# Attention followed by a squared-ReLU layer: filler count, order of the v load, two-part AV and an undrained batch change

## The chip, the cores and the metric

The kernel runs on one core of one Trainium2 chip. Its engines are TensorE (PE, the matmuls; PEld is its weight load, which runs beside the matmuls), VectorE (DVE), ScalarE (ACT), GpSimd (POOL) and SyncE (SP, which issues DMAs). The metric is device time of one launch in microseconds (us), the median of several runs. A profile is taken from one execution; its span is the time from the first to the last instruction.

## The reference

```
scores = (q @ k^T) / sqrt(64)            # 8 batches, 16 query heads, 4 key heads, 384 tokens, 64 wide
attn   = softmax(scores)
x      = (attn @ v), heads side by side  # 3072 x 1024
h      = relu(x @ w_in)                  # w_in 1024 x 2048
out    = (h * h) @ w_out                 # w_out 2048 x 1024
```

## The kernel before, in words

A *pair* is two query heads of one batch that share a key head; a batch has 8 pairs, and there are 64 pairs, numbered n = 0 to 63. The feed-forward part of a batch is 16 *up* chunks (x times 128 columns of w_in, L616) and two *down* halves of w_out, each with three row tiles (L642).

Three styles of code follow one another.

**The first batch (the prologue)** is cut into 24 units (one pair by 128 queries) and is ordered by a small planner (L107). Each task has an assumed duration, an earliest time (K_AT, Q_AT, V_AT at L794 to L796 say when loads are taken to have landed; W_AT and B_AT when further loads are issued) and takes buffers from pools. The planner's output is a static order for each engine. Where TensorE's assumed clock shows a gap, the hook `between` (L861) puts in *fillers*: matmuls on a zero tile (L313) whose results nobody reads. A unit is: scores (L395), exp on ScalarE (L406), AV (L422, attention weights times v, with a column of ones that gives the row sums), and for each two units a division (L431, L433) and a transpose back (L332, L444). The first 4 up chunks of batch 0 are done here for each of three row tiles t (L447: four matmul groups into PSUM bank `f_ps[0]`, then relu L460 and square L465). Keys and queries are cast (L300, L305) and transposed on TensorE (L332, L340). The first loads are issued by hand on SP and ACT (L278 to L287): k of group 0, q of pairs 0 and 1, k of the other groups, v, then q of pairs 2-3, 4-5, 6-7.

**From batch 1 on** TensorE is used as two halves of 64 rows, *lo* and *hi*, that work at the same time: every product is cut into pieces for the lower and the upper 64 rows of the contraction. `push` (L502) emits the lo pieces at once and keeps the hi pieces in the list `behind`; `catch_up` (L482) emits them among later lo pieces, at the earliest GAP = 450 ns of assumed clock after the lo pieces end, since the hi pieces add to the same PSUM bank and the first of them waits for the last lo piece. A job marked urgent goes ahead of others. `drain` (L525) emits all hi pieces that are left, with no lo work beside them. `both` (L518) emits pieces on both halves. `next_bank` (L535) hands out four PSUM banks in rotation (`rota`).

For each pair n there are: first half of its scores (L545; three matmuls into banks 0 to 2, then one exp L557 over the three), second half of its scores into the same three banks, so that it has to wait for the first exp; AV of pair n-1 (`row_attend`, L561: 18 lo pieces, then 18 hi pieces, all into the one bank `po`, then reciprocal L575 and multiplication L577 on VectorE, which free `po` and fill `o_sb`); and steps of the feed-forward part, taken one by one from the generator `ffn` (L740). An up step ends in relu (L629) and a square; a down tile is computed in three steps of 6, 5 and 5 matmuls per half for each of three tiles, after which VectorE copies it out (L664).

**Batch 1** (n = 8 to 15, L882 to L895) has a hand-written order per pair: first scores, one ffn step, `row_turn(n-2)` (L591: o_sb transposed on TensorE, then copied to xT at L607), AV of pair n-1, second scores, one ffn step. The 16 ffn steps are the 12 up chunks of batch 0 that are left and the first four steps of its first down half (9 steps in all).

**The batch change** (n = 16, L896 to L904): AV of pair 15, ffn step, turn of pair 14, ffn step, turn of pair 15, then `fill(LULL)` takes ffn steps for 6000 ns, then `drain()`, and only then the scores of pair 16. From there pairs go on with `fill(ahead)` and `fill(per - ahead)` (2200 and 2800 ns) between the halves of the scores; transposes are done by DMA. The keys and queries of batch 2 are transposed by DMAs from SP (L359, L366), issued in pair 13. After the last pair the rest of the feed-forward part runs with full 128-row matmuls (L684, L703).

Of the kernel before, what the change touches and what calls it, by code (L numbers as in the profile page):

```python
# [165 lines left out]
def bass_gqa_attention__then__ffn_squared_relu_kernel(  # L166
# [106 lines left out]
    def first_q(c0, c1, queue):  # L273
# [6 lines left out]
    first_q(1, 2, "sync")  # L280
    first_k(1, 4)
    R.add("sync", lambda e: e.dma_start(
        v_f.ap().rearrange("p g j d -> p g (j d)"), v[0].rearrange("g (p j) d -> p g (j d)", j=NJ)),
        writes=["v_f"], dma="vf")
    first_q(2, 4, "sync")
    first_q(4, 6, "sync")
# [153 lines left out]
    def unit_turned(u, bank):  # L440
# [4 lines left out]
              reads=[key], writes=[("xT", 0, c, t), ("xT", 0, c + 1, t)])  # L445

    def unit_up(t, c):  # L447
        acc, key = f_ps[0].ap(), ("f_ps", 0)

        def mm(pe):  # L450
            for kc in range(NKC):
                m = pe.matmul(acc[:, c * 128:(c + 1) * 128], w_in_sb[:, kc, c * 128:(c + 1) * 128],  # L452
                              xT[0][:, kc, t * 128:(t + 1) * 128], start=(kc == 0), stop=(kc == NKC - 1))
            return m

        R.add("tensor", mm, reads=[("w_in", c * 128 // WC)] + [("xT", 0, kc, t) for kc in range(NKC)], writes=[key])

    def unit_relu(t):
        acc, key = f_ps[0].ap(), ("f_ps", 0)
        R.add("vector", lambda e: e.tensor_scalar_max(hq[t % 2][:, :], acc, 0.0),  # L460
              reads=[key], writes=[("hq", t % 2)] + under(t % 2))
# [69 lines left out]
    held = set()  # L531
    rota = [0, 1, 2, 3]
    po_owner = []
# [26 lines left out]

    def row_attend(p, then=None):  # L561
        b, g = p // NPB, (p % NPB) // 2
# [21 lines left out]

        while po_owner and not po_owner[-1]["over"]:
            clock["lo"] += 100.0
            catch_up(clock["lo"])
        lo, hi = ([piece(r, f, j) for f in range(2 * NJ) for j in range(NJ)] for r in range(2))
        po_owner.append(push(lo, hi, done, urgent=True)[0])

    def row_turn(p):  # L591
        b, c = p // NPB, p % NPB
        i = next_bank()
        acc, key = F_BANKS[i]
        ps = acc.bitcast(bf16)
# [18 lines left out]
        owner[i], total = push(lo, hi, done, urgent=True)  # L614

# [202 lines left out]
    for u in range(NU):  # L818
# [6 lines left out]
        if c % 2 == 0:  # L825
            acc = {}
        av[u] = P.task(on_pe(0.19), lambda e, h, u=u, ex=slot: unit_attend(u, h["bank"], ex["exp"]), 1 + u * 0.01,
                       [a, v_cast] + ([av[u - 1]] if c % 2 else []), take=[] if c % 2 else ["bank"],
                       give=[("exp", slot)], hold=acc)
        if c % 2:  # L830
# [8 lines left out]
                       give=[("bank", b2), ("ob", o)], hold=b2)  # L839
            a["give"].append(("bank", acc))  # L840
            turned_at[t].append(x)
    done = None
    W_LAND = 15.0
    for t in range(NJ):
        up_hold, hq_hold, a = {}, {}, None
        for c in range(4):
            a = P.task(on_pe(0.45), lambda e, h, t=t, c=c: unit_up(t, c), 20 + t, turned_at[t] + ([a] if a else []),
                       take=[] if c else ["up"], hold=up_hold, at=W_LAND if c < 2 else W_LAND + 2.8)
        a = P.task({DVE: (0.69, 0.03)}, lambda e, h, t=t: unit_relu(t), 13, [a], take=["hq"], give=[("up", up_hold)],
                   hold=hq_hold)  # L850
        P.task({POOL: (1.05, 0.03)}, lambda e, h, t=t: unit_square(t), 5, [a], give=[("hq", hq_hold)], hold=hq_hold)
# [21 lines left out]
    for n in range(NPB, NP + 1):  # L873
# [78 lines left out]
```

## Time and profile before

| | |
|---|---|
| median of 3 runs | 433.91 us (433.33 to 434.0) |
| the profiled execution | 433.79 us |
| its span, first to last instruction | 431.9 us |
| TensorE busy | 423.8 us (98%) |
| VectorE, ScalarE, GpSimd busy | 166.7, 198.0, 60.8 us |
| first scores of pair 8 (end of the prologue) | 33.20 us after the span's start |
| second scores of pair 16 | 81.41 us |

A timeline row reads: start, duration, engine, line, operation, output<-inputs, shape, count of merged instructions; in brackets the idle time of the engine before it and what ended it. A row of a waits view reads: who <- whom: us in total, times, longest. In a groups view the figures after the bar are busy us and mean ns of one. Matmul ends are modelled, so a matmul row is longer than the time it keeps others out: starts are the better measure.

### The profile page before, as it was taken

The numbers are of one execution on the slowest core, as the hardware profiler recorded it, in microseconds if no ns is written. First come the engines' busy times: TensorE is split into PE (matmuls) and PEld (weight loads), VectorE is DVE, ScalarE is ACT, GpSimd is POOL, SyncE is SP. The second block draws the span as 40 slices with busy tenths as digits, with TensorE's granted clock in tenths as the row PEclk, the third lists the DMA queues.
The fourth block names the chain that finished last, engine by engine and source line by source line (L and its number), as shares of the span: only waits on it lengthen the run. The fifth ranks groups of instructions, "written<-read, shape, count | busy, mean of one in ns | idle before, by whom it ended". The sixth has DMA issues, their size and how long they took to land.

```text
span 431.9 us, 13352 instructions
## 1 busy us (share of the span) xinstructions
PE 423.8 (98%) x6173; PEld 319.9 (74%) x6173; DVE 166.7 (39%) x364; ACT 198.0 (46%) x250; POOL 60.8 (14%) x75
## 2 busy tenths in 40 slices
PE   8999998899999999999999999999999999999997
PEld 6786675678878888888788887888878888746544
DVE  4773543242333442344422543334423444224412
ACT  4945550565333564436644565445654466003300
POOL 4927350021000300022000300021000000000000
PEclk9999999999999999999999999999999999999999
DMA  7999999139521990249603992239902210120012
GB/s 218 178 197 201 202 190 184 43 34 153 157 69 61 132 175 20 93 103 147 94 20 94 115 184 45 80 63 171 123 20 94 83 21 20 45 97 26 0 61 86
DMA packets 92792, 44.25 MB, mean 102 GB/s; under 512 B 71104, under 2 KB 86720, under 8 KB 92736
## 3 DMA queue, kind: packets, MB, share of 16 engines
q0 software_dynamic: 34288, 16.65, 30.9%
q1 hardware_dynamic: 58176, 26.55, 29.3%
q8 instruction: 48, 0.79, 0.7%
q10 hardware_dynamic: 272, 0.20, 0.1%
q14 instruction: 8, 0.07, 0.1%
HBM read 35.65 MB, written 12.58 MB: 112 GB/s over the span
## 4 chain that ended last, share of the span: by engine, by line
PE 93%; DVE 2%; ACT 2%; DMA 2%; SPq 0%; issue 0%
PE f_ps L655 15%; PE f_ps L623 15%; PE sc_ps L655 14%; PE sc_ps L623 14%; PE po L567 11%; PE f_ps L703 7%; PE sc_ps L553 7%; PE f_ps L684 5%; DMA q_f<-in_q_dram 2%; ACT expT L557 2%; PE f_ps L452 1%; PE sc_ps L395 1%; PE po L422 0%; PE f_ps L332 0%; PE f_ps L422 0%; DVE q_f L664 0%
## 5 line engine op out<-in xcount | busy, mean ns | idle before, releaser
L557 ACT ACTIVATE expT<-sc_ps 128x1152 bf16<-128x1152 f32 x112 | 126.2, 1126 | 99.9 <-PE sc_ps L553 50.0
L623 PE MATMUL sc_ps<-xT,w_in_sb 64*128 64x384 bf16 x864 | 133.8, 322 | 0.4 <-DVE q_f L664 0.4
L655 PE MATMUL f_ps<-w_out_sb,h2T 64*128 64x512 bf16 x640 | 131.7, 376 | 0.0
L623 PE MATMUL f_ps<-xT,w_in_sb 64*128 64x384 bf16 x864 | 130.7, 323 | 0.2 <-DVE q_f L664 0.2
L655 PE MATMUL sc_ps<-w_out_sb,h2T 64*128 64x512 bf16 x608 | 128.2, 376 | 0.0
L623 PEld LDWEIGHTS f_ps<-xT,w_in_sb 64*128 64x128 bf16 x864 | 71.3, 94 | 16.1 <-DVE q_f L664 0.9
L623 PEld LDWEIGHTS sc_ps<-xT,w_in_sb 64*128 64x128 bf16 x864 | 71.4, 94 | 15.5 <-DVE q_f L664 0.9
L635 ACT ACTIVATE h2T<-hr 128x384 bf16<-128x384 f32 x96 | 50.1, 522 | 71.5 <-DVE hr L629 71.5
L567 PE MATMUL po<-v_aug,expT 64*128 64x65 bf16 x2016 | 81.4, 190 | 1.0 <-DVE o_sb L577 1.0
L567 PEld LDWEIGHTS po<-v_aug,expT 64*128 64x128 bf16 x2016 | 75.9, 94 | 8.7 <-DVE o_sb L577 1.3
L655 PEld LDWEIGHTS f_ps<-w_out_sb,h2T 64*128 64x128 bf16 x640 | 56.0, 94 | 12.5 <-PE sc_ps L655 0.6
L655 PEld LDWEIGHTS sc_ps<-w_out_sb,h2T 64*128 64x128 bf16 x608 | 54.4, 94 | 12.0 <-PE f_ps L655 0.3
L553 PE MATMUL sc_ps<-qT,kT 64*128 64x384 bf16 x336 | 55.2, 323 | 1.7 <-ACT expT L557 1.2
L575 DVE RECIPROCAL rinv<-po 128x6 f32<-128x6 f32 x56 | 11.0, 196 | 104.4 <-PE f_ps L655 47.4
L629 DVE TENSOR_SCALAR hr<-sc_ps 128x384 f32<-128x384 f32 x54 | 30.0, 556 | 36.2 <-PE sc_ps L623 24.0
L629 DVE TENSOR_SCALAR hr<-f_ps 128x384 f32<-128x384 f32 x54 | 30.1, 558 | 33.6 <-PE f_ps L623 19.5
L577 DVE TENSOR_TENSOR o_sb<-po,rinv 128x384 bf16<-128x384 f32 x56 | 31.2, 557 | 1.9
L703 PE MATMUL f_ps<-w_out_sb,h2T 128*128 128x512 bf16 (+2 forms) x160 | 31.5, 358 | 0.0
L553 PEld LDWEIGHTS sc_ps<-qT,kT 64*128 64x128 bf16 x336 | 23.8, 94 | 8.4 <-ACT expT L557 5.2
L234 POOL DMA_DIRECT2D k_st<-in_k_dram x7 | 5.3, 760 | 170.2 <-DMA xT<-o_sb 170.2
L703 PEld LDWEIGHTS f_ps<-w_out_sb,h2T 128*128 128x128 bf16 x160 | 15.0, 98 | 16.5 <-DVE q_f L664 0.4
L693 ACT ACTIVATE h2T<-hr 128x384 bf16<-128x384 f32 x16 | 8.4, 523 | 33.7 <-DVE hr L691 33.7
(84 smaller groups left out, 253.0 us busy)
## 6 DMA issues: line engine op xcount, KB each, us to landing
out_dram<-q_f SPq DMA_DIRECT2D x47, 256.0 KB, 2.3
q_st<-in_q_dram POOLq DMA_DIRECT2D x7, 768.0 KB, 11.1
w_in_sb<-in_moe_w_in_dram POOLq DMA_DIRECT2D x8, 512.0 KB, 14.5
w_out_sb<-in_moe_w_out_dram POOLq DMA_DIRECT2D x2, 2048.0 KB, 23.2
k_st<-in_k_dram POOLq DMA_DIRECT2D x7, 192.0 KB, 4.5
v_st<-in_v_dram POOLq DMA_DIRECT2D x7, 192.0 KB, 10.8
q_f<-in_q_dram SPq DMA_DIRECT2D x3, 384.0 KB, 7.4
xT<-o_sb SPq DMA_TRANSPOSE x48, 2.7
```

Of the source, the lines that this page charges most:

```text
L553: "tensor", lambda pe: pe.matmul(sc_ps[:, i, 0:S], kt[rows, j * 128:(j + 1) * 128], qt[rows, :]),
L557: R.add("scalar", lambda e: e.activation(expT[p % NEX][:, 3 * half:3 * half + 3, :], sc_ps[:, 0:3, 0:S], AF.Exp, scale=0.125), reads=[("sc ...
L567: "tensor", lambda pe: pe.matmul(po_v[:, f % NJ, f // NJ, :], expT[p % NEX][rows, 2 * j + f % 2, f // 2 * 128:f // 2 * 128 + 128], v_aug[b ...
L575: R.add("vector", lambda e: e.reciprocal(rinv_v, po_v[:, :, :, D:D + 1]), reads=["po"], writes=[("rinv", p % 2)])
L577: R.add("vector", lambda e: e.tensor_tensor(o_sb[p % NO][:, :, :, :], po_v[:, :, :, 0:D], rinv_v.to_broadcast([128, NJ, 2, D]), ALU.mult), ...
L623: "tensor", lambda pe: pe.matmul(acc[:, 0:S], w_in_sb[rows, kc, c * 128:(c + 1) * 128], xT[b % NXT][rows, kc, :], start=(h == 0 and kc == ...
L629: R.add("vector", lambda e: e.tensor_scalar_max(hr[r][:, :], acc[:, 0:S], 0.0), reads=[key], writes=[("hr", r)])
L635: R.add("scalar", lambda e: e.activation(h2T[b % 2][:, c, :], hr[r][:, :], AF.Square), reads=[("hr", r)], writes=[("h2T", b % 2, c, t) for ...
L655: "tensor", lambda pe: pe.matmul(acc, h2T[b % 2][rows, c, i * 128:(i + 1) * 128], w_out_sb[rows, c, jj * 512:(jj + 1) * 512], start=(h == ...
L684: m = pe.matmul(acc[:, 0:S], w_in_sb[:, kc, c * 128:(c + 1) * 128], xT[b % NXT][:, kc, :], start=(kc == 0), stop=(kc == NKC - 1))
L693: R.add("scalar", lambda e: e.activation(h2T[b % 2][:, c, :], hr[r][:, :], AF.Square), reads=[("hr", r)], writes=[("h2T", b % 2, c, t) for ...
L703: m = pe.matmul(f_ps[u][:, 0:c1 - c0], h2T[b % 2][:, c, i * 128:(i + 1) * 128], w_out_sb[:, c, jj * 512 + c0:jj * 512 + c1], start=(c == 0 ...
```

## The change

- **Fillers.** Eight instead of six at the start; the planner's TensorE clock is then set to 2.8 us instead of staying at 1.4. In gaps before 5.2 us a filler counts as 0.22 us, later as 0.11; before, 0.13 throughout.
- **Loads.** The load of v is issued after that of q pairs 2-3. The planner's landing times for k, q and v and the issue time of w_in are set later (v at 9.1 instead of 6.9; q pairs 2-3 at 7.85 instead of 8.2).
- **Planner.** A pool `acc` of two limits how many AV accumulators hold a bank at once. The up chunks of the last row tile (t = 2) go to bank 3 of `sc_ps` instead of `f_ps[0]`; the rotation starts at bank 1 accordingly.
- **AV of batch 1's loop in two parts.** `row_attend(p, part=0)` does 9 lo and 9 hi pieces, `part=1` the other 9 and 9 after them, then the division. The order per pair is: first scores, ffn step, AV part 0 of n-1, second scores, turn of n-2, ffn step, AV part 1 of n-1.
- **Batch change.** Two ffn steps, turn of 14, AV of 15 (whole), two ffn steps, turn of 15 into the bank `po`, `fill(LULL)`; no drain.

```diff
     first_k(1, 4)
+    first_q(2, 4, "sync")
     R.add("sync", lambda e: e.dma_start(
         v_f.ap()...
-    first_q(2, 4, "sync")
...
+    def up_bank(t):
+        return (f_ps[0].ap(), ("f_ps", 0)) if t < NJ - 1 else (sc_ps[:, 3], ("sc", 3))
+
     def unit_up(t, c):
-        acc, key = f_ps[0].ap(), ("f_ps", 0)
+        acc, key = up_bank(t)
...
     def unit_relu(t):
-        acc, key = f_ps[0].ap(), ("f_ps", 0)
+        acc, key = up_bank(t)
...
-    rota = [0, 1, 2, 3]
+    rota = [1, 2, 3, 0]
...
-    def row_attend(p, then=None):
+    def row_attend(p, then=None, part=None):
...
-        while po_owner and not po_owner[-1]["over"]:
-            clock["lo"] += 100.0
-            catch_up(clock["lo"])
-        lo, hi = ([piece(r, f, j) for f in range(2 * NJ) for j in range(NJ)] for r in range(2))
-        po_owner.append(push(lo, hi, done, urgent=True)[0])
-
-    def row_turn(p):
+        if part != 1:
+            while po_owner and not po_owner[-1]["over"]:
+                clock["lo"] += 100.0
+                catch_up(clock["lo"])
+        heads = range(NJ) if part == 0 else range(NJ, 2 * NJ) if part == 1 else range(2 * NJ)
+        lo, hi = ([piece(r, f, j) for f in heads for j in range(NJ)] for r in range(2))
+        prev = po_owner.pop() if part == 1 else None
+        po_owner.append(push(lo, hi, None if part == 0 else done, prev, urgent=True)[0])
+
+    def row_turn(p, home=None):
         b, c = p // NPB, p % NPB
-        i = next_bank()
-        acc, key = F_BANKS[i]
+        if home is None:
+            i = next_bank()
+        acc, key = home or F_BANKS[i]
...
+    P.pool("acc", range(2))
...
-    K_AT = (3.3, 5.6, 5.6, 5.6)
-    Q_AT = (3.9, 4.5, 8.2, 8.2, 9.4, 9.4, 10.6, 10.6)
-    V_AT = 6.9
+    K_AT = (3.3, 6.2, 6.2, 6.2)
+    Q_AT = (3.9, 4.5, 7.85, 7.85, 10.35, 10.35, 11.6, 11.6)
+    V_AT = 9.1
...
-    W_AT, B_AT = 7.0, 12.0
+    W_AT, B_AT = 8.0, 12.0
...
         if eng == PE and was < 16.0 and begin - was > 0.3:
-            idle(int((begin - was - 0.1) / 0.13))
-
-    idle(6)
+            idle(int((begin - was - 0.1) / (0.22 if was < 5.2 else 0.11)))
+
+    idle(8)
+    P.clock[PE] = 2.8
...
             row_scores(n, 0)
             next(ffn)
+            if n > NPB:
+                row_attend(n - 1, part=0)
+            row_scores(n, 1)
             if n > NPB + 1:
                 row_turn(n - 2)
+            next(ffn)
             if n > NPB:
-                row_attend(n - 1)
-            row_scores(n, 1)
-            next(ffn)
+                row_attend(n - 1, part=1)
...
         if n == 2 * NPB:
+            next(ffn)
+            next(ffn)
+            row_turn(n - 2)
             row_attend(n - 1)
             next(ffn)
-            row_turn(n - 2)
             next(ffn)
-            row_turn(n - 1)
+            row_turn(n - 1, (po.ap(), "po"))
             ready[0] = 1
+            credit[0] = 0.0
             fill(LULL)
-            drain()
```

More of the change, by code (lines that the diff above doesn't have):

```diff
@@ L613, in row_turn @@
             catch_up(clock["lo"])
-        owner[i], total = push(lo, hi, done, urgent=True)
+        job, total = push(lo, hi, done, urgent=True)
+        if home is None:
+            owner[i] = job
     def row_up(b, c, r):
@@ L827, in bass_gqa_attention__then__ffn_squared_relu_kernel @@
         av[u] = P.task(on_pe(0.19), lambda e, h, u=u, ex=slot: unit_attend(u, h["bank"], ex["exp"]), 1 + u * 0.01,
-                       [a, v_cast] + ([av[u - 1]] if c % 2 else []), take=[] if c % 2 else ["bank"],
+                       [a, v_cast] + ([av[u - 1]] if c % 2 else []), take=[] if c % 2 else ["bank", "acc"],
                        give=[("exp", slot)], hold=acc)
@@ L839, in bass_gqa_attention__then__ffn_squared_relu_kernel @@
                        give=[("bank", b2), ("ob", o)], hold=b2)
-            a["give"].append(("bank", acc))
+            a["give"] += [("bank", acc), ("acc", acc)]
             turned_at[t].append(x)
@@ L847, in bass_gqa_attention__then__ffn_squared_relu_kernel @@
             a = P.task(on_pe(0.45), lambda e, h, t=t, c=c: unit_up(t, c), 20 + t, turned_at[t] + ([a] if a else []),
-                       take=[] if c else ["up"], hold=up_hold, at=W_LAND if c < 2 else W_LAND + 2.8)
-        a = P.task({DVE: (0.69, 0.03)}, lambda e, h, t=t: unit_relu(t), 13, [a], take=["hq"], give=[("up", up_hold)],
-                   hold=hq_hold)
+                       take=["up"] if c == 0 and t < NJ - 1 else [], hold=up_hold, at=W_LAND if c < 2 else W_LAND + 2.8)
+        a = P.task({DVE: (0.69, 0.03)}, lambda e, h, t=t: unit_relu(t), 13, [a], take=["hq"],
+                   give=[("up", up_hold)] if t < NJ - 1 else [], hold=hq_hold)
         P.task({POOL: (1.05, 0.03)}, lambda e, h, t=t: unit_square(t), 5, [a], give=[("hq", hq_hold)], hold=hq_hold)
```

## The prediction, made before the changed kernel ran

> **What bounds the kernel now.** I read the page first, then the waits of TensorE, then a table of stretches, then the timeline row by row where that table shows TensorE short of work.
>
> ```profile
> span 431.9 us, 13352 instructions
> PE 423.8 (98%) x6173; PEld 319.9 (74%) x6173; DVE 166.7 (39%) x364; ACT 198.0 (46%) x250; POOL 60.8 (14%) x75
> PE 93%; DVE 2%; ACT 2%; DMA 2%; SPq 0%; issue 0%
> ```
>
> TensorE is the bound: no other engine is half busy, and 93% of the chain that ended last is its own. So the change can only win where TensorE waits or runs one half alone. The execution took 433.79 us, 1.9 us more than its span; the median is 433.91, so the sum below holds for either.
>
> ```profile
> 33.20:63.05 29.85, 29.42 (x537) 20.04 (x536) 13.65 (x30) 16.97 (x15) 18.10 (x20) 1.00 1.36 203
> 63.05:81.41 18.36, 15.18 (x205) 9.10 (x199) 6.24 (x13) 3.72 (x5) 0.00 (x0) 1.00 0.88 144
> 81.41:102.00 20.59, 20.59 (x337) 16.36 (x339) 8.21 (x17) 12.97 (x19) 4.20 (x4) 1.00 0.60 56
> ```
>
> The columns are the stretch, its length, and the busy time of PE, PEld, DVE, ACT and POOL. From 81.41 on TensorE is full, and nothing of the change acts there. The stretch of the batch change (second scores of pair 15 to second scores of pair 16) has 3.2 us without any matmul. The loop of batch 1 looks full, but a busy half counts as busy, so I check it by starts below.
>
> **Part 1, the prologue.** Engines are mixed in this timeline of before:
>
> ```profile
> 1.05 4.96 PE L316 MATMUL f_ps<-warm 128*128 128x256 bf16 x24 [1.05 <-DVE tiny L290]
> 3.28 0.55 DVE L305 CAST k_dup<-k_f 128x384 bf16<-128x384 f32 x1 [2.28 <-DMA k_f<-in_k_dram]
> 5.85 0.33 PE L332 MATMUL sc_ps<-ident,k_dup 128*128 128x128 bf16 x3
> 6.90 0.51 PE L395 MATMUL sc_ps<-qT,kT 64*128 64x128 bf16 x12
> 7.29 3.65 ACT L406 ACTIVATE expT<-sc_ps 128x768 bf16<-128x768 f32 x5 [4.57 <-PE sc_ps L395]
> 8.37 0.83 POOL L309 CAST v_aug<-v_f 128x768 bf16<-128x768 f32 x1 [1.06 <-DMA v_f<-in_v_dram]
> 9.54 1.05 DVE L300 CAST q_st<-q_f 128x384 bf16<-128x384 f32 x2 [0.78 <-DMA q_f<-in_q_dram]
> 21.80 4.83 ACT L406 ACTIVATE expT<-sc_ps 128x768 bf16<-128x768 f32 x6 [0.18 <-PE sc_ps L395]
> 31.31 1.96 PE L452 MATMUL f_ps<-xT,w_in_sb 128*128 128x128 bf16 x32 [0.26 <-DVE q_f L460]
> ```
>
> The first keys are cast at 3.83, but their transpose starts at 5.85, since 24 fillers stand ahead of it: 4.8 us for 24 is 0.20 us each, where the planner counted 0.13. In the changed kernel the planner's gap from 2.8 to the cast's planned end at 3.95 takes (1.15 - 0.1)/0.22 = 4 fillers, 12 in all. At 0.21 us each they end at 3.6, and the transpose starts when the cast is done, about 3.9. From there to the first exp before took 7.29 - 5.85 = 1.44 us; at the slow pace and with the query's transpose behind its cast I take 2.0, so the first exp comes at 5.9, **1.4 us earlier**.
>
> Not all of that arrives. Two pairs give six units, which last the exps from 5.9 to about 10.7 (24 exps end at 26.63, so 0.81 apart). Queries 2-3 now load in the place of v: they land near 8.3 instead of 9.5, so they come in time, but v lands near 9.5 instead of 8.3, so with a cast of 0.83 the first AV starts near 10.4, where before the cast had ended at 9.2. Two AVs are thus owed, the planner assumes both landings 0.4 us too early, and TensorE executes in order, so it stands at them. I take 0.5 us off. Against that, the own bank of t = 2 removes the 0.26 us wait at 31.31 for the relu of t = 1. Sum: 1.4 - 0.5 + 0.2 = **1.1 us gained**, from 0 (the AVs owed cost the lead) to 2.0 (all of it, and half of the exps' idle time between). The pool of two accumulators I cost at nothing: an AV that it delays is covered by the 9 exp buffers.
>
> [...]
>
> ```profile
> L316 PE MATMUL f_ps<-warm 128*128 128x256 bf16 x20 | 4.4, 420 | 1.1 <-DVE tiny L290 1.1
> L316 PE MATMUL f_ps<-warm 128*128 128x256 bf16 x3 | 0.5, 272 | 0.0
> ```
>
> The first row (from 1 to 5.2 us) has fillers of 420 ns, the second (at 6.2 us) the same ones at 272 ns, so TensorE ran slow until about 5.5 us. The changed kernel leaves gaps of up to 0.3 us unfilled from 3.6 on. [...]
>
> **Part 2, batch 1's loop.** One full pair of before, TensorE, ScalarE and VectorE:
>
> ```profile
> 46.28 0.29 PE L567 MATMUL po<-v_aug,expT 64*128 64x65 bf16 x4
> 46.81 0.32 PE L553 MATMUL sc_ps<-qT,kT 64*128 64x384 bf16 x1
> 47.45 1.13 ACT L557 ACTIVATE expT<-sc_ps 128x1152 bf16<-128x1152 f32 x1 [1.23 <-PE sc_ps L623]
> 48.41 0.20 DVE L575 RECIPROCAL rinv<-po 128x6 f32<-128x6 f32 x1 [0.71 <-PE f_ps L623]
> 48.64 0.56 DVE L577 TENSOR_TENSOR o_sb<-po,rinv 128x384 bf16<-128x384 f32 x1
> 48.63 0.49 PE L553 MATMUL sc_ps<-qT,kT 64*128 64x384 bf16 x3
> 50.35 0.29 PE L567 MATMUL po<-v_aug,expT 64*128 64x65 bf16 x4
> 52.71 0.49 PE L553 MATMUL sc_ps<-qT,kT 64*128 64x384 bf16 x3
> ```
>
> ```profile
> 36.64 0.50 PE sc_ps L553 x3
> 40.48 0.50 PE sc_ps L553 x3
> 60.82 0.50 PE sc_ps L553 x3
> 81.91 1.30 PE sc_ps L623 x16
> 103.78 1.08 PE f_ps L655 x10
> ```
>
> From first scores to first scores is 52.71 - 48.63 = 4.08 us. The work of one half: an up step is 1.30 (16 pieces on two halves, in the chain of waits), the scores 0.49, AV 18 x 0.033 = 0.59, a turn 0.09; with two up steps 3.77. So **0.31 us a pair is lost**, and the rows say where: second scores at 46.81, exp at 47.45 for 1.13, next first scores at 48.63. This round trip of 1.82 us has only one up step beside it.
>
> The split moves half an AV (0.30) and the turn into that gap: 0.16 + 0.09 + 1.30 + 0.30 = 1.85, so that wait goes. **But a new one comes.** Part 0 of the next pair writes the same bank `po` and must wait for the division, and this distance shrinks. Before, from AV start to AV start there were 50.35 - 46.28 = 4.07 us, of which the round trip needs 49.20 - 46.28 = 2.92. At the batch change the trace shows that it can bite:
>
> ```profile
> 62.54 0.22 PE L567 MATMUL po<-v_aug,expT 64*128 64x65 bf16 x2
> 65.03 0.56 DVE L577 TENSOR_TENSOR o_sb<-po,rinv 128x384 bf16<-128x384 f32 x1
> 65.65 0.20 PE L567 MATMUL po<-v_aug,expT 64*128 64x65 bf16 x1 [1.04 <-DVE o_sb L577]
> ```
>
> Here two AVs stand close, and the second starts 3.11 us after the first, with 1.04 us of idle TensorE. Half an AV takes 0.30 off the lo run and 0.30 off the hi run, not off the gap between them nor off VectorE's 0.79: from part 1 to the next part 0 it needs 2.39 (from 2.92, and 0.06 to get back) to 2.52 (from 3.11). What stands between is 0.30 + 0.32 + 1.30 = 1.92. So TensorE waits 0.47 to 0.60 us in each pair; I take 0.50. Queued behind the waiting piece are the rest of the AV and the second scores, on both halves, so it is a plain loss. Part 1's own wait for part 0's last hi piece costs nothing: 1.4 us needed, 1.85 there. A pair then takes 3.77 + 0.50 = **4.27 instead of 4.08**.
>
> Counted over the loop: pair 8 is unchanged; pair 9 (40.48 - 36.64 = 3.84) has no division ahead and takes 0.32 + 1.30 + 0.30 + 0.16 + 1.30 + 0.30 = 3.68 or a little more, 0.14 less; pairs 10 to 14 took 60.82 - 40.48 = 20.34 and will take 21.35; pair 15 up to its second scores (at 63.05) took 2.23 and will take 1.62 + 0.50 + 0.30 = 2.43. **1.05 us lost**, where a split without the new wait would gain 1.8.
>
> **Part 3, the batch change.**
>
> ```profile
> 69.01 0.20 PE L601 MATMUL sc_ps<-ident,o_sb 64*128 64x64 bf16 x1 [0.36 <-DVE xT L607]
> 72.89 0.33 PE L623 MATMUL sc_ps<-xT,w_in_sb 64*128 64x384 bf16 x1 [0.38 <-DVE q_f L664]
> 78.39 0.33 PE L553 MATMUL sc_ps<-qT,kT 64*128 64x384 bf16 x1
> 80.25 1.11 ACT L557 ACTIVATE expT<-sc_ps 128x1152 bf16<-128x1152 f32 x1
> 81.41 0.50 PE L553 MATMUL sc_ps<-qT,kT 64*128 64x384 bf16 x3 [1.23 <-ACT expT L557]
> ```
>
> The work of one half between the two second scores: scores 0.16 and 0.32, six down steps at 1.08, AV 0.59, two turns 0.18, four up steps 5.20: 12.93 us of 18.36, so **5.43 us are lost**. Named: 1.04 (AV of 15 at `po`), 0.36, 0.38, and 1.23 for the exp, which came late because drained squares stood ahead of it on ScalarE and only one up step stood between the score halves. The other 2.4 is one half working alone, in the drain above all.
>
> In the new order AV of 15 has two down steps ahead of it (2.46 against 2.39 needed: no wait), turn of 15 has two after the AV (0.59 + 2.16 = 2.75 against 3.05: 0.3 us of wait, new, since it needs `o_sb` and `po`); the first up chunk needs the copied xT only at its last piece, 2.2 us after the turn, where some 1.4 is enough. No up step waits for a copied-out down bank, since the turn no longer takes one and four up steps spread the rest. After LULL two up steps (2.6) stand between the score halves instead of one, more than the 1.82 needed. The same work then takes 12.93 + 0.3, and 0.39 for half an AV and a turn that now fall behind the mark: 13.62, **4.74 us gained**. The credit line does nothing, since credit is 0 there already.
>
> What could come late instead is the DMA of batch 2's queries:
>
> ```profile
> 62.03 10.21 SPq L366 DMA_TRANSPOSE qT<-q_st  x2
> DMA to landing us min/median/max: 11.0/11.0/11.0
> ```
>
> The first transpose lands at 73.0; pair 16's first scores move from 78.39 to about 76, so 3 us are left.
>
> **Sum:** 433.79 - 1.1 + 1.05 - 4.74 = **429.0 us**.
>
> **The rivals.**
> *The division is no wait* (hi pieces or VectorE quicker than in the rows): the loop gains 1.8 instead of losing 1.05, 426.2. For it: 0.31 a pair is there to be had. Against: 2.92 and 3.05 in the rows above. Chance 0.20.
> *The batch change does not do what it says*: only the waits of 1.04 and 1.23 go, and what the drain cost comes back as waits for banks and xT. 433.79 - 1.1 + 1.05 - 2.3 = 431.4. Chance 0.13.
> *The prologue's lead is lost* at the later v: 430.1, chance 0.08. With the second rival at once, and 0.60 for each wait in the loop, 433.1: within the noise, chance 0.06.
> *Slower: TensorE does not reach full pace in the prologue.* Its work there, counted by starts, is about 19 us of the 27.3 from 5.9 to 33.2 (24 units and 24 transposes with 0.17 for a group, 12 up groups at 0.45). At half pace all of it takes 38 us, and the loop begins 9 to 11 us later: 439. The point: x us at half pace cost 0.29x, so slower than before needs some 19 us of it. For it: 272 against 420 ns above. Against: full pace came after 4.5 us, and the new gaps are short. [...]
>
> **How the numbers follow.** The forecast has 0.45. The range 425.6 to 431.6 takes in the forecast with both ends of part 1, the wait from 0 to 0.60, and the first three rivals (0.86); the last two cases lie outside. A measurement of this kernel tells about 0.2% (0.9 us) from no change. Faster: 0.45 + 0.20 + 0.13 + 0.08 = 0.86; same 0.06; slower 0.08.
>
> **What would show it.** First exp near 5.9 and first scores of pair 8 near 32.1; rows of L567 with a wait of about 0.5 on DVE o_sb L577 in pairs 10 to 15, and 4.27 from first scores to first scores; no wait of the second scores of pair 16 for the exp. A period of 3.8 would make part 2 wrong, a wait on DMA qT part 3, fillers' pace lasting beyond 6 us part 1.

## The result, and the profile after

The changed kernel took **430.19 us** (median of 6 runs, 429.58 to 430.39) against 434.04 for the kernel before on the same chip (6 runs, 433.33 to 435.27): the medians are 3.85 us apart, and the ratio is 0.9903, 95% interval 0.9886 to 0.9920, so about 1% faster. The forecast was 429.0 with a range of 425.6 to 431.6. The sign and the size are right, but three terms of the sum are not. Their errors (1.1 and 0.8 us too much gained, 0.76 too much lost) cancel in part, so that the sum came within 1.2 us is in part luck. The profiled execution took 430.17 us.

The first three lines of the page after, as they stood for before (length; busy time of the engines; the chain that ended last):

```profile
span 428.3 us, 13436 instructions
PE 421.3 (98%) x6215; PEld 329.9 (77%) x6215; DVE 167.3 (39%) x366; ACT 197.7 (46%) x250; POOL 59.5 (14%) x73
PE 92%; DMA 4%; DVE 2%; SPq 1%; issue 0%; ACT 0%; POOL 0%
```

TensorE is still the bound. DMA has 4% of the chain instead of 2%; half of that are the keys of batch 1 (below). The stretches after, cut at the same first and second scores as those of before (columns: stretch, length, busy time of PE, PEld, DVE, ACT, POOL):

```profile
33.22:63.37 30.15, 28.83 (x524) 21.19 (x523) 13.90 (x32) 16.95 (x15) 17.98 (x20) 1.00 1.36 202
63.37:80.33 16.96, 16.46 (x247) 11.28 (x244) 6.79 (x14) 3.94 (x6) 0.00 (x0) 1.00 1.07 157
80.33:102.00 21.67, 21.67 (x344) 18.14 (x342) 8.77 (x18) 13.69 (x20) 4.21 (x4) 1.00 0.55 60
```

The second row must be read with its counts: 16.96 against 18.36 us looks like 1.40 gained, but it holds 247 matmuls where before held 205. The second scores of pair 16 now stand behind two more up steps (2.6 us of work), so this mark has moved within the work, and the gain shows only when the stretch is taken to the end of the execution. The table does that; "first scores of 8" is the first matmul of batch 1's loop, the loop ends with the second scores of pair 15, and the last column is the time from there to the span's end.

| kernel | first exp | last exp of batch 0 | first scores of 8 | loop | rest |
|---|---|---|---|---|---|
| before | 7.29 | 25.82 | 33.20 | 29.86 | 368.89 |
| after | 6.08 | 25.32 | 33.22 | 30.15 | 364.97 |
| difference | -1.21 | -0.50 | +0.02 | +0.29 | -3.92 |
| forecast | -1.4 | | -1.1 | +1.05 | -4.74 |

So the whole gain is the batch change. The prologue's lead is there at its beginning and gone at its end. ScalarE's exps of batch 0 show the way (start, duration of the group, count, idle time before and its releaser):

```profile
6.08 5.05 ACT L406 ACTIVATE expT<-sc_ps 128x768 bf16<-128x768 f32 x7 [3.36 <-PE sc_ps L395]
11.30 9.22 ACT L406 ACTIVATE expT<-sc_ps 128x768 bf16<-128x768 f32 x12 [0.16 <-PE sc_ps L395]
21.74 1.51 ACT L406 ACTIVATE expT<-sc_ps 128x768 bf16<-128x768 f32 x2 [1.22 <-PE sc_ps L395]
23.63 1.51 ACT L406 ACTIVATE expT<-sc_ps 128x768 bf16<-128x768 f32 x2 [0.38 <-PE sc_ps L395]
25.32 0.81 ACT L406 ACTIVATE expT<-sc_ps 128x768 bf16<-128x768 f32 x1 [0.18 <-PE sc_ps L395]
```

The last of the twelve starts at 11.30 + 9.22 - 0.81 = 19.71; the same exp, the nineteenth, started at 21.80 before. The lead had grown to 2.1 us, and then 1.22 us of it went at once, at 20.5. What stands there, first in the waits by row, then in the chain that ended last:

```profile
19.87 0.56 DVE L352 COPY k_dup<-k_st 128x1536 bf16<-128x1536 bf16 x1 [1.50 <-DMA k_st<-in_k_dram]
20.69 0.29 PE L332 MATMUL f_ps<-ident,ob 128*128 128x128 bf16 x2 [1.02 <-DVE xT L444]
```

```profile
11.70 8.15 DMA k_st<-in_k_dram
19.85 0.02 issue
19.87 0.56 DVE k_dup L352
```

VectorE comes to the copy of batch 1's keys at 18.37, because everything ahead of it now runs earlier; the planner's due time for it (K1_AT = 19.0) is as before, and the keys land at 19.85. Their load is issued 1.17 us earlier than before (11.70 against 12.87), but it takes 8.15 us where it took 6.7, so it lands no earlier. The same load takes 8.0 to 8.4 us in E4, E5 and E6, 6.4 to 6.6 with the old prologue (E2, E3, E8) and 7.0 with v asked for first again (E10), so the new order of the loads seems to make it longer; by what way is not shown. VectorE stands for 1.50 us, and the copies and divisions of batch 0 that follow in its order start only behind this copy (20.35, 20.55, 20.75); TensorE then stands for 1.02 us at a transpose of `ob`, and ScalarE for 1.22 us for its scores.

In the loop the new wait is there. One pair, TensorE and VectorE:

```profile
48.30 0.22 PE L570 MATMUL po<-v_aug,expT 64*128 64x65 bf16 x2
48.58 0.48 PE L556 MATMUL sc_ps<-qT,kT 64*128 64x384 bf16 x3
48.99 0.25 PE L570 MATMUL po<-v_aug,expT 64*128 64x65 bf16 x3
49.24 0.19 PE L570 MATMUL po<-v_aug,expT 64*128 64x65 bf16 x1
49.73 0.20 DVE L578 RECIPROCAL rinv<-po 128x6 f32<-128x6 f32 x1 [0.26 <-PE f_ps L632]
49.96 0.56 DVE L580 TENSOR_TENSOR o_sb<-po,rinv 128x384 bf16<-128x384 f32 x1
50.58 0.23 PE L570 MATMUL po<-v_aug,expT 64*128 64x65 bf16 x2 [0.17 <-DVE o_sb L580]
52.71 0.48 PE L556 MATMUL sc_ps<-qT,kT 64*128 64x384 bf16 x3
```

Part 1 starts at 48.30 with its lo pieces, its hi pieces run from 48.99 to 49.43, the division ends at 50.52, part 0 of the next pair starts at 50.58. The pair takes 52.71 - 48.58 = 4.13 us (4.08 before, 4.27 forecast).

And the batch change has no drain, but waits that the forecast ruled out:

```profile
71.14 0.69 DVE L673 COPY q_f<-sc_ps 128x512 f32<-128x512 f32 x1 [0.92 <-PE po L608]
71.89 0.33 PE L632 MATMUL sc_ps<-xT,w_in_sb 64*128 64x384 bf16 x1 [0.27 <-DVE q_f L673]
```

The first up chunk starts at 71.89, 0.06 after the copy of a down bank (71.14 + 0.69 = 71.83): it was given the bank that this copy empties. The turn of 15 waits for its division, by the waits of TensorE's weight loads (total us, times, longest):

```profile
PEld po L608 <- DVE o_sb L580: 0.6, 1, 0.6
```

All stretches below come from profiled executions, and the two whose mean granted clock was 0.95 (E1's and E7's) are not used for them, only to see where a wait stands. Ratios are against the kernel before on the same chip.

### The profile page after: what moved, and what is told of

Same layout as the page of the kernel before. It is cut to its first block, busy times and chain, and to the rows that moved or that the text cites. A ratio compares the mean times of both kernels' runs of the same rounds, so it can differ in the third digit from the quotient of the medians.

```text
span 428.3 us, 13436 instructions
## 1 busy us (share of the span) xinstructions
PE 421.3 (98%) x6215; PEld 329.9 (77%) x6215; DVE 167.3 (39%) x366; ACT 197.7 (46%) x250; POOL 59.5 (14%) x73
## 4 chain that ended last, share of the span: by engine, by line
PE 92%; DMA 4%; DVE 2%; SPq 1%; issue 0%; ACT 0%; POOL 0%
PE sc_ps L664 16%; PE f_ps L664 15%; PE f_ps L632 15%; PE sc_ps L632 14%; PE po L570 12%; PE sc_ps L556 7%; PE f_ps L693 5%; PE f_ps L712 5%; DMA k_st<-in_k_dram 2%; DMA q_f<-in_q_dram 2%; DVE o_sb L580 1%; PE f_ps L455 1%; PE sc_ps L455 0%; SPq L274 0%; DVE q_f L673 0%; DVE rinv L578 0%
## 5 line engine op out<-in xcount | busy, mean ns | idle before, releaser
L632 PE MATMUL sc_ps<-xT,w_in_sb 64*128 64x384 bf16 x864 | 147.4, 323 | 0.3 <-DVE q_f L673 0.3
L664 PE MATMUL sc_ps<-w_out_sb,h2T 64*128 64x512 bf16 x704 | 145.7, 376 | 0.0
L632 PE MATMUL f_ps<-xT,w_in_sb 64*128 64x384 bf16 x864 | 141.8, 322 | 0.1
L664 PE MATMUL f_ps<-w_out_sb,h2T 64*128 64x512 bf16 x640 | 137.5, 376 | 0.0
L632 PEld LDWEIGHTS sc_ps<-xT,w_in_sb 64*128 64x128 bf16 x864 | 76.3, 94 | 11.5 <-DVE q_f L673 1.0
L570 PE MATMUL po<-v_aug,expT 64*128 64x65 bf16 x2016 | 83.7, 190 | 1.2 <-DVE o_sb L580 1.2
L632 PEld LDWEIGHTS f_ps<-xT,w_in_sb 64*128 64x128 bf16 x864 | 74.4, 94 | 10.7 <-DVE q_f L673 0.5
L664 PEld LDWEIGHTS sc_ps<-w_out_sb,h2T 64*128 64x128 bf16 x704 | 62.2, 94 | 14.4 <-PE f_ps L664 0.3
L673 DVE COPY q_f<-sc_ps 128x512 f32<-128x512 f32 x22 | 15.2, 690 | 24.8 <-PE sc_ps L664 18.0
L693 PE MATMUL f_ps<-xT,w_in_sb 128*128 128x384 bf16 x128 | 21.0, 326 | 0.0
```

The source lines that it names most:

```text
L570: "tensor", lambda pe: pe.matmul(po_v[:, f % NJ, f // NJ, :], expT[p % NEX][rows, 2 * j + f % 2, f // 2 * 128:f // 2 * 128 + 128], v_aug[b ...
L632: "tensor", lambda pe: pe.matmul(acc[:, 0:S], w_in_sb[rows, kc, c * 128:(c + 1) * 128], xT[b % NXT][rows, kc, :], start=(h == 0 and kc == ...
L664: "tensor", lambda pe: pe.matmul(acc, h2T[b % 2][rows, c, i * 128:(i + 1) * 128], w_out_sb[rows, c, jj * 512:(jj + 1) * 512], start=(h == ...
L673: R.add("vector", lambda e: e.tensor_copy(y_sb[yb][:, :], acc), reads=[key], writes=[("y", yb, 0)] + under(2 + yb))
L693: m = pe.matmul(acc[:, 0:S], w_in_sb[:, kc, c * 128:(c + 1) * 128], xT[b % NXT][:, kc, :], start=(kc == 0), stop=(kc == NKC - 1))
```

## The experiments

**E1: the prologue's edits alone.** The changed kernel with the loop and the batch change of before:

```diff
-            if n > NPB:
-                row_attend(n - 1, part=0)
-            row_scores(n, 1)
             if n > NPB + 1:
                 row_turn(n - 2)
-            next(ffn)
             if n > NPB:
-                row_attend(n - 1, part=1)
+                row_attend(n - 1)
+            row_scores(n, 1)
+            next(ffn)
```

(and `if n == 2 * NPB:` as before.)

> Before, with only the edits of the prologue (fillers, order of the v load, planner times, accumulator pool, own bank for the last up chunks). Theory A (the lead of the early exps is given back whole to the stand of VectorE at the keys of batch 1): the first scores of pair 8 at 33.2, the time within 0.3 us of before. My prediction's term: 1.1 us faster. If the edits cost time by themselves: slower by more than 0.3 us.

Measured: 434.88 against 433.95, ratio 1.0027 [1.0011, 1.0044]. The prologue's edits alone gain nothing; they cost 0.5 to 1.9 us. E8 below removes them from the changed kernel and finds no difference, so the two disagree by about 1 us on how much they cost; on their gaining nothing they agree. E1's trace shows a wait of about this size far behind the prologue, where the code goes over to full-width matmuls:

```profile
390.07 10.73 PE L712 MATMUL f_ps<-w_out_sb,h2T 128*128 128x512 bf16 x47 [1.01 <-DVE q_f L673]
```

Before, after and E8 have no such wait of TensorE there. So E1's cost may come from the shifted start of the bank rotation, which is one of its edits, and not from the prologue; this was not tested.

**E2: the split alone.** The kernel before with the loop order of the changed one (`row_attend` in parts).

```diff
+            if n > NPB:
+                row_attend(n - 1, part=0)
+            row_scores(n, 1)
             if n > NPB + 1:
                 row_turn(n - 2)
-            if n > NPB:
-                row_attend(n - 1)
-            row_scores(n, 1)
             next(ffn)
+            if n > NPB:
+                row_attend(n - 1, part=1)
```

> Before, with only AV in two parts in batch 1's loop and the new order of the pair. Reading of the changed kernel's rows (a wait of some 0.35 us at po in six pairs instead of 0.31 at the exp): 4.13 us from first scores to first scores, 0 to 0.4 us slower than before. My prediction's term: 1.05 slower. Rival, the division is no wait: 3.8 us a pair and 1.8 us faster. The old batch change follows it here, so AV of 15 stands at po as before.

Measured: 434.33 against 433.95, ratio 1.0008 [0.9993, 1.0023]; the loop takes 30.14 us (before 29.86, after 30.15). So by the profiles the split costs 0.3 us, and does so without the rest of the change; the timed runs (-0.3 to +1.0 us) can't tell it from nothing, but rule out a gain of 1.8.

**E3: the batch change alone.** The kernel before with only the new block at `n == 2 * NPB`.

```diff
         if n == 2 * NPB:
+            next(ffn)
+            next(ffn)
+            row_turn(n - 2)
             row_attend(n - 1)
             next(ffn)
-            row_turn(n - 2)
             next(ffn)
-            row_turn(n - 1)
+            row_turn(n - 1, (po.ap(), "po"))
             ready[0] = 1
+            credit[0] = 0.0
             fill(LULL)
-            drain()
```

> Before, with only the new order at the batch change (two steps between turns and AV, the last turn into po, no drain). From the changed kernel's rows: 3.6 to 4.2 us faster. My prediction's term, 4.74, is too large by the waits for copied-out banks and for the last turn that the changed kernel shows. Rival (the waits come back in full): 2.3 faster.

Measured: 429.53 against 433.95, ratio 0.9891 [0.9875, 0.9908]. From the second scores of pair 15 to the end it takes 365.12 us, 3.77 less than before (368.89). This one block carries the whole gain. It also shows the wait at the down banks, with 0.70 us:

```profile
71.68 0.33 PE L629 MATMUL sc_ps<-xT,w_in_sb 64*128 64x384 bf16 x1 [0.70 <-DVE q_f L670]
```

**E4: the copy of batch 1's keys planned later.** The changed kernel with one number changed:

```diff
-    K1_AT, Q1_AT, V1_AT = 19.0, 22.5, 23.5
+    K1_AT, Q1_AT, V1_AT = 20.8, 22.5, 23.5
```

> The changed kernel, with one number changed: the planner takes the keys of batch 1 to land at 20.8 instead of 19.0, so that VectorE comes to their copy four to six instructions later. Theory A (this copy stood 1.5 us for its load with all of VectorE's queue behind it, and gave back the lead of 2.1 us): no such stand, first scores of pair 8 at 31.2 to 32.0, 1.2 to 2.0 us faster than the changed kernel, about 428.5. Rival B (the lead is lost to the AVs that the later v leaves owed, or TensorE's own work sets the end): the stand goes, the first scores of pair 8 stay at 33 and the time stays at 430.2.

Measured: 429.33 against 433.95, ratio 0.9890 [0.9875, 0.9905]; first scores of pair 8 at 32.26 instead of 33.22.

```profile
20.51 1.47 POOL L352 COPY k_dup<-k_st 128x1536 bf16<-128x1536 bf16 x1 [0.57 <-DMA k_st<-in_k_dram]
32.26 0.49 PE L556 MATMUL sc_ps<-qT,kT 64*128 64x384 bf16 x3
```

With the later due time the planner puts the copy on GpSimd, where it waits 0.57 us with nothing of batch 0 behind it. So the wait of VectorE for the keys ate a part of the lead: 0.95 us comes back in the profiles, less than the 1.2 to 2.0 expected. The timed intervals of after and E4 overlap (their ratios are 0.6 us apart), and E4's prologue ends at 31.60 to 32.58 in five profiles (E4, E5, E6, E11, E12); all five lie ahead of the 33.22 of after, of which there is one profile.

**E5: E4, and the AV undivided and last in the pair.** The order of the loop becomes:

```diff
             row_scores(n, 0)
             next(ffn)
-            if n > NPB:
-                row_attend(n - 1, part=0)
             row_scores(n, 1)
+            next(ffn)
             if n > NPB + 1:
                 row_turn(n - 2)
-            next(ffn)
             if n > NPB:
-                row_attend(n - 1, part=1)
+                row_attend(n - 1)
```

> As e4_k1_later, but AV of batch 1's loop is whole again and stands last in its pair, after the turn: first scores, step, second scores, step, turn of n-2, AV of n-1. Theory (two round trips set the pair: 1.72 to 1.82 us from score half to score half, and 2.9 us from AV to the next AV less what is split off): po is free long before the next AV, and between first and second scores stand 1.62 us, so 0.1 to 0.2 us are lost per pair instead of 0.36: 3.87 to 3.97 us a pair, 0.9 to 1.6 us faster than e4, ratio to before about 0.986. Rival (the split loses nothing that a whole AV would not): a pair of 4.1, no faster than e4.

Measured: 427.90 against 433.87, ratio 0.9859 [0.9843, 0.9875]. The loop takes 28.53 instead of 30.15 us, the way from there to the first scores of pair 16 14.57 instead of 14.13: 1.18 us gained, with no AV waiting for the division. The largest wait that is left is that of TensorE's weight loads for the exp (total us, times, longest):

```profile
PEld sc_ps L556 <- ACT expT L560: 3.0, 9, 0.5
```

**E6: E4, and the bank of the turn of pair 14 put first in the rotation** at the batch change, so that the first up chunk takes this one, empty for long by then, and the down steps' banks come one chunk later:

```diff
             row_turn(n - 2)
+            rota.insert(0, rota.pop())
             row_attend(n - 1)
```

> As e4_k1_later, but at the batch change the bank that the turn of pair 14 has used comes to the front of the rotation, so that the first up chunk of batch 1 takes it and not the bank of a down tile that VectorE still copies out. Theory (the 0.7 us that the batch change lacks against my sum are the waits for copied-out banks and for the last turn): the waits on the copy go, 0.3 to 0.7 us faster than e4 in the stretch from second scores of pair 15 to second scores of pair 16, that is 16.3 to 16.7 instead of 16.96. Rival (they stand beside one half's work and cost nothing): 16.9.

Measured: 428.29 against 433.87, ratio 0.9869 [0.9850, 0.9888]. From the second scores of pair 15 to the first of pair 16 it takes 13.28 us where E4 takes 14.13: 0.85 gained. Of TensorE's waits between 33 and 90 us this row alone remains; those for `q_f` are gone:

```profile
PE po L570 <- DVE o_sb L580: 1.2, 6, 0.4
```

**E7: E4, E5 and E6 together.**

> All three: keys of batch 1 later, whole AV last in its pair, the turn's bank first. If the three are independent: the sum of what e5 and e6 gain over e4, 1.2 to 2.3 us, ratio to before about 0.985, and faster than both kernels.

Measured: 428.05 against 433.87, ratio 0.9861 [0.9843, 0.9878]. By the timed runs it is no better than E5. Its trace has no wait for a copied-out bank at the batch change, but one of 1.3 us (weight load) at the end of the half-row code, at L693, where E5 and E6 have 0.4: this is where E6's gain went (see E12).

**E8: the changed kernel with the prologue of before** (fillers, due times, v, the last up chunk's bank), that is, E2 and E3 together.

> Before, with the split and the batch change but none of the prologue's edits. Theory A (the prologue's edits as they stand bring nothing or cost up to 0.5 us): 0 to 0.7 us faster than the changed kernel, ratio to before 0.989 to 0.991. Rival (the prologue's edits gain my 1.1 us): 1 us slower than the changed kernel, ratio 0.9925 or more.

Measured: 430.02 against 433.87, ratio 0.9907 [0.9892, 0.9923]; first scores of pair 8 at 33.26, the loop 30.15, the rest 364.97. It is the changed kernel's time (430.19) without any of the prologue's edits.

**E9: E4 with the fillers of before**, to see whether they carry what E4 gained:

```diff
-            idle(int((begin - was - 0.1) / (0.22 if was < 5.2 else 0.11)))
+            idle(int((begin - was - 0.1) / 0.13))

-    idle(8)
-    P.clock[PE] = 2.8
+    idle(6)
```

> As e4_k1_later, but with the fillers of before (six at the start, 0.13 us counted for one, TensorE's planned clock not moved). Theory (the filler count alone makes the lead): first exp at 6.5 to 7.9 as in the kernels with the old prologue, first scores of pair 8 at 32.8 to 33.4 instead of 32.1, 0.7 to 1.2 us slower than e4, ratio to before about 0.9915. Rival (the load order and the planner's times carry the gain): first scores of pair 8 within 0.3 us of e4's.

Measured: 430.38 against 434.08, ratio 0.9923 [0.9902, 0.9944]: 1.05 us over E4's median (the two intervals just overlap), so the lead that E4 lets through needs the fewer fillers. Its profiled execution lost more, for a reason of its own (last section).

**E10: E4 with v asked for first again**, queries 2-3 behind it, and the planner's times to match:

```diff
-    first_q(2, 4, "sync")
     R.add("sync", lambda e: e.dma_start(
...
         writes=["v_f"], dma="vf")
+    first_q(2, 4, "sync")
...
-    Q_AT = (3.9, 4.5, 7.85, 7.85, 10.35, 10.35, 11.6, 11.6)
-    V_AT = 9.1
+    Q_AT = (3.9, 4.5, 9.1, 9.1, 10.35, 10.35, 11.6, 11.6)
+    V_AT = 7.85
```

> As e4_k1_later, but the load of v is asked for ahead of that of q pairs 2-3 again, with the planner's two times exchanged. My prediction's step (the later v leaves AVs owed and takes 0.5 us off the lead): first AV near 9.0 instead of 10.3, and first scores of pair 8 0.3 to 0.7 us earlier than e4's 32.1. Rival (the earlier queries are worth more than the earlier AVs, since without them the exps run dry after six units): a gap of 0.3 us or more in the exps near 10, first scores of pair 8 no earlier or up to 0.5 later.

Measured: 430.16 against 434.08, ratio 0.9910 [0.9890, 0.9931]; first scores of pair 8 at 33.35, against 32.26 in E4. The exps run dry, for longer than before the change (0.29 us at 11.23 there):

```profile
9.91 0.81 ACT L406 ACTIVATE expT<-sc_ps 128x768 bf16<-128x768 f32 x1 [0.17 <-PE sc_ps L395]
11.35 2.26 ACT L406 ACTIVATE expT<-sc_ps 128x768 bf16<-128x768 f32 x3 [0.63 <-PE sc_ps L395]
```

The exp of 9.91 ends at 10.72, and the one at 11.35 has waited 0.63 us for scores of pair 2, whose queries came late. So the later v does not cost the lead; it gains 1.1 us in the profiles and 0.8 in the medians (the two intervals overlap). Running dry is only a part of it: at the last exp of batch 0 E10 is 0.37 us behind E4 (25.05 against 24.68), and the other 0.72 comes between there and the first scores of pair 8. Since E9 and E10 each give back about 1 us, neither the fillers nor the order of the loads carries the lead alone.

**E11: E7, and one more down step ahead of the last turn**, so that the turn of 15 needn't wait for its division:

```diff
             next(ffn)
             next(ffn)
+            next(ffn)
             row_turn(n - 1, (po.ap(), "po"))
```

> As e7_k1_av_bank, but with three down steps instead of two between AV of pair 15 and its turn. The rows of the changed kernel have the turn waiting for the division of AV 15; with 1.08 us more ahead of it that wait goes, and the first up chunk then stands 0 to 0.2 for the copied xT. Theory: 0.2 to 0.5 us faster than e7, near 427.5, ratio to before 0.984 to 0.985. Rival (the copied xT is late instead): as e7.

Measured: 428.24 against 434.08, ratio 0.9867 [0.9849, 0.9885]. The wait comes back at another place, since the first up steps need the xT that this turn yields; TensorE's weight loads between 60 and 90 us:

```profile
PEld f_ps L632 <- DVE xT L614: 0.8, 1, 0.8
```

Up to the first scores of pair 16 it now takes 15.42 us. Of this 1.08 is the added step, so 14.34 is to be set against E5's 14.57. The timed runs show no gain over E7 (428.05). Work put between division and turn is taken away between turn and up step.

**E12: E7, and the turns one pair later, between the halves of the scores**, to give the exp more time:

```diff
             next(ffn)
+            if n > NPB + 2:
+                row_turn(n - 3)
             row_scores(n, 1)
             next(ffn)
-            if n > NPB + 1:
-                row_turn(n - 2)
```

(with `row_turn(n - 3)` between the first two `next(ffn)` at the batch change.)

> As e7_k1_av_bank, but the turn stands between first and second scores, one pair later (of n-3, since that of n-2 would find its division unfinished); the turn of pair 13 moves to the batch change. Theory (the score half's round trip of 1.72 to 1.82 us is the only wait left in the loop, and 1.62 us stood beside it): 0.09 more stands beside it, a pair goes from 3.91 in e5 to 3.82 to 3.85. And the bank in front, whose effect e7's timing left open, shows in the waits: no up chunk waits for a copied-out bank, second scores of pair 15 to first scores of pair 16 in 13.8 to 14.0 instead of e5's 14.57. Together 0.8 to 1.4 us faster than e5, ratio to before 0.983 to 0.984. Rival (a turn in the way delays the second scores by what it fills): 3.91 a pair and the ratio of e5, 0.986.

Measured: 427.64 against 433.80, ratio 0.9859 [0.9841, 0.9877]. The loop takes 27.75 us, 0.78 less than E5, and the waits for the exp fell by half:

```profile
PEld sc_ps L556 <- ACT expT L560: 1.4, 4, 0.5
```

The expected 0.983 to 0.984 did not come, since 0.85 us is given back far behind, at the first full-width up step. The waits of weight loads there, in E12 and in E5:

```profile
PEld f_ps L693 <- DVE q_f L673: 1.3, 1, 1.3
```

```profile
PEld f_ps L693 <- DVE q_f L673: 0.4, 1, 0.4
```

E12's rows show what it waits for:

```profile
381.14 0.69 DVE L673 COPY q_f<-f_ps 128x512 f32<-128x512 f32 x1 [0.39 <-PE f_ps L664]
381.89 6.35 PE L693 MATMUL f_ps<-xT,w_in_sb 128*128 128x384 bf16 x38 [0.79 <-DVE q_f L673]
```

The copy of the last down tile ends at 381.83, and the step starts 0.06 after it, as at the batch change: it is given the bank that VectorE has still to empty. In E5 the last tile stands in a bank of `sc_ps`. E7 and E11 have the same wait of 1.3 us, so the turn's bank in front gains at the batch change and, together with E5's loop, loses it at the other end of the rotation; no run took this wait away. E5, E7 and E12 can't be told apart by their times (427.64 to 428.05); all three beat both kernels, by about 6 us against before and about 2 against after.

## Why the prediction was right in its sum, and where its steps failed

**Part 1, the prologue (forecast -1.1, measured 0).** The fillers did what was forecast: keys' transpose at 3.99 (forecast 3.9), first exp at 6.08 (5.9). The sum failed behind that. The step "Two AVs are thus owed ... I take 0.5 us off" named the wrong culprit: E10 moves v back to the front and is 1.1 us worse at the first scores of pair 8. What ate the lead first is a wait that the forecast had not on its list: the copy of batch 1's keys, planned at a fixed time ahead of VectorE's other work, which an earlier prologue reaches before its DMA has landed (1.50 us of VectorE, 1.22 of the exps). E4 moves that copy alone and gains 0.95 us in the profiles. The rival "the prologue's lead is lost" gave 430.1, which is what came, but with v as its reason.

That is not all of it: E4 leads by 1.64 us at the nineteenth exp (20.16), and by 0.94 at the first scores of pair 8. Of these 0.70 us, 0.50 go up to the last exp of batch 0, where the exps wait 0.20, 0.18 and 0.29 us for their scores, and 0.20 behind it. The rows of the transposes (L332) from there to those scores, before, after and in E4:

```profile
25.82:33.20 7.38, 2.87 (x33) 1.00 1.46 198
```

```profile
25.32:33.22 7.90, 4.23 (x46) 1.00 1.46 198
```

```profile
24.68:32.26 7.58, 3.87 (x44) 1.00 1.46 198
```

From the last exp to the first scores of pair 8 it is 7.90 instead of 7.38 us, with 46 transposes there instead of 33 (the columns are stretch, length, busy time and count of that line); in E4 it is 7.58 with 44. This stretch hardly varies: it is 7.38 or 7.39 in E2, E3 and E8 too, and 7.59 in E5 and E6. In the planner's new order more of batch 1's transposes stand behind the last exp. Thirteen transposes at 0.055 us each (0.11 for two in the chain) are 0.7 us, less 0.26 for a wait that is gone; this part is read off the rows and wasn't tested alone. The own bank of the last up chunks did what was forecast (the 0.26 us wait at 31.31 is gone).

**Part 2, the loop (forecast +1.05, measured +0.29).** The mechanism is the one forecast, the division's wait at `po` in pairs 10 to 15; its size was off. Forecast: 2.39 to 2.52 us needed from part 1 to the next part 0, 1.92 of work between, a wait of 0.47 to 0.60. Measured: 50.58 - 48.30 = 2.28, so 0.36, and 3.77 + 0.36 = 4.13 is the measured pair. The needed distance came from two rows where a whole AV had run, less 0.59 for half of its lo and half of its hi run; the rows of after give it directly as 0.69 from the lo to the hi run, 0.44 for the hi run, 0.30 to the reciprocal, 0.79 for VectorE and 0.06. The bounds were too high by 0.11 to 0.24, and the measured wait lies below both ends of the stated 0.47 to 0.60. Over pairs 10 to 14 that is 5 x 0.14 = 0.7 of the 0.76 us by which the term was off. That the wait, and not the split itself, is the price follows from the pair's sum; E5, where the loop falls by 1.62, takes away both at once and can't tell them apart.

**Part 3, the batch change (forecast -4.74, measured -3.92).** The drain is gone, and so is its wait for the exp. The step "No up step waits for a copied-out down bank, since the turn no longer takes one and four up steps spread the rest" is false: the rotation hands out the bank that was taken longest ago and is no longer held. A down step's three banks are taken at its beginning and held to its end, so at its end they stand at the front, though VectorE has not copied them out; the turn's bank, empty for long, stands at the back. Against E4, E6 changes that order alone, and from the second scores of pair 15 to the end it needs 13.28 + 350.87 = 364.15 us, which is 4.74 less than before: the term, though that the two agree to the hundredth is chance. The wait of the turn of 15 (forecast 0.3) is there with up to 0.6 in its weight load, and in E11 one more step in between moves it to another place.

**The sum.** By the two profiles 0.02 + 0.29 - 3.92 = -3.61, the difference of their spans (428.34 - 431.95); -3.85 by the timed runs (the ratio's interval of 0.9886 to 0.9920 is -4.9 to -3.5 us). The rival "slower" (TensorE not reaching full pace, 0.08) came in no median; in the profile after, three transposes of keys take 0.50 us at 3.99 and 0.34 at 7.22, the later figure as before (0.34 at 7.34). "The division is no wait" fell by the rows at 50.58; "the batch change does not do what it says" by E3.

## What to carry to other kernels

When work is moved earlier, look in every engine's order for the first instruction with a fixed due time behind it that waits for a DMA: here VectorE stood 1.50 us at one, a good part of the lead ended there, and giving that one instruction to an idle engine brought 0.95 us. When a rotation of banks meets a change of order, write down which bank each step is given and who empties it last, up to the end of the rotation: in E7 what was won at one end was lost at the other. And compare stretches by the work in them: here a mark moved past two up steps, and a gain of 3.92 us read as 1.40.

## What the runs showed of the hardware

**The pace of TensorE in the first microseconds differed from execution to execution: 4.22 to 5.30 us for the same 24 fillers.** Before's row stands in the prediction (4.96 us), E8 and E9 took 5.30; here E2 and E3:

```profile
1.05 4.22 PE L316 MATMUL f_ps<-warm 128*128 128x256 bf16 x24 [1.05 <-DVE tiny L290]
```

```profile
1.05 5.00 PE L316 MATMUL f_ps<-warm 128*128 128x256 bf16 x24 [1.05 <-DVE tiny L290]
```

With the prologue of before the first exp came at 7.29, 6.54, 7.32 and 7.85 (before, E2, E3, E8), with the new one between 5.70 and 6.22. The first scores of pair 8 vary too, and not in step with it: E4, E6 and E5 have the same prologue, with first exps at 6.00, 5.79 and 5.92, and reach them at 32.26, 32.45 and 31.60. So a single profile can't tell 0.5 us in a prologue, while behind the batch change the same code agrees within 0.02 us (364.97 in the rest for after and for E8). The pace shows in the starts of the fillers: in before, 17 of them start between 1.05 and 4.65 us, 0.21 apart, and three between 6.19 and 6.52, 0.11 apart, about twice the rate. The change comes near 5.5 us in before. In E2 it comes near 4.0, an estimate: the transpose behind the 24 starts at 5.11, and the 4.06 us from 1.05 on hold some 14 fillers at 0.21 and 10 at 0.11. In E8 and E9 it does not come within the 24 (5.30 us, 0.22 each). The granted clock reads 1.00 in these first microseconds of before, after and E9, so that column does not show the slow pace.

**The granted clock fell in the middle of E9's prologue, to 0.61 and 0.54 over two stretches of 2 us.** The profiled execution (stretch, length, TensorE's busy time and count, granted clock), and the stand ahead of it:

```profile
18.00:20.00 2.00, 1.23 (x25) 1.00 1.57 186
20.00:22.00 2.00, 1.94 (x30) 0.61 1.61 193
22.00:24.00 2.00, 2.00 (x33) 0.54 1.56 194
24.00:26.00 2.00, 2.00 (x41) 1.00 1.47 197
```

```profile
18.77 0.34 PE L395 MATMUL sc_ps<-qT,kT 64*128 64x128 bf16 x5 [0.83 <-issue]
```

TensorE stood for 0.83 us, for nothing that the profile shows, and was busy for 1.23 of 2.00; then it was granted 0.61 and 0.54 of full speed over these two stretches (in slices of half a microsecond, 0.50 from 20.5 to 23.5). Six score matmuls take 0.50 us at 20.44, 0.34 at 19.45. The first scores of pair 8 came at 35.79, some 3 us late. Three microseconds at a granted 0.50 are an estimated 1.5 us of lost work; the stand is another 0.83. Another timed execution of E9 had the same time (433.66 and 433.50, the other eight 429.22 to 431.82) and the same mean clock of 0.996; so had one of 12 executions of E1 (436.57 us) and one of 23 of before (435.53). So it is rare (four of the 45 executions of these three kernels) and not E9's own; that the stand was its cause is argued from the order of the rows and was not tested.
